# Sliding-window attention into a feed-forward block: one set of eight PSUM banks, score groups of five blocks, and v copies in one piece

## The chip, the core and the metric

The kernel runs on one core of a Trainium2 chip, in one launch. Its time is device microseconds (us). The kernel before was run 11 times: median 265.92 us, from 264.36 to 268.71. The engines are named as the profile names them: PE is TensorE (its matmuls; PEld is its weight loads), DVE is VectorE, ACT is ScalarE, POOL is GpSimd, SP is SyncE.

## What is computed

The reference, cut to what matters (B = 8 batches, H = 8 heads, S = 576 positions, D = 64; 4608 tokens of d_model 512, d_ff 1024):

```
rel = pos[:, None] - pos[None, :]
mask_plain = (rel >= 0) & (rel < 32)                       # heads 0..3
mask_dil = (rel >= 0) & (rel < 128) & (rel % 4 == 0)       # heads 4..7
scores = where(mask, q @ k.T / 8, -1e9)
attn = exp(scores - max);  attn = attn / (sum(attn) + 1e-9)
x = (attn @ v), heads side by side: (4608, 512)
h = (x @ w1) * (x @ w2) @ w3
out = h @ w_out                                            # (4608, 512), f32
```

## The kernel before

**How the work is cut.** Heads 0 to 3 (u=0, plain window) and 4 to 7 (u=1, dilated, rearranged so that its window is plain too) are cut into six blocks of 96 queries, each against 128 keys. Three blocks of four heads are one *step* `b.i` (i = 2u + half), so a batch has four steps and the kernel 32. The feed-forward part takes units of 288 tokens (two per batch, k = 0 to 15), and w3 and w_out are multiplied into one matrix `wf` first, so that a unit needs x@w1, x@w2, their product, and one more matmul.

**The tasks**, with the lines of the profile (line numbers of the kernel before):

- `T`: DVE transposes rows of q, k (and v of batches 0 and 1) into `qt`, `kt`, `vt` (L296, L309).
- `S`: scores on PE into `sp` (L365), 24 matmuls of 32 rows by 96 columns, four at a time in the four row strips of the array. In batches 0 and 1 (`BIASED`) four matmuls first put the mask in as a bias (L348); later batches mask after the exponential.
- `E`: the exponential on ACT, `sp` to `et` (L375). `M`: the mask multiply on DVE (L381), batches 2 to 7.
- `VT`, `VK`: for batches 0 and 1, PE transposes v (L318) and ACT (L329) or DVE (L331) copies it to `vp`, in three pieces per half; `VKE` says which engine. Later batches load v into `vp` by DMA (`LP`, `LD`: L206, L220) and DVE copies the overlap (`HALO`, L227).
- `V`: attention times v on PE, two tasks of 6 matmuls per step (L398). `R`, `N`: reciprocal and normalisation on DVE (L416, L427).
- The result goes to `XT`, transposed: in batches below `TURNED` by PE (`X`, L444) and a copy on ACT (`K`, L451); in the others by a transposing DMA from SP's queue (`XD`, L454).
- `A`, `B`: x@w1 and x@w2 of a unit, 4 matmuls for each of 8 column blocks (L473); `CA` copies A on ACT (L484), `G` multiplies on DVE (L489). `Y`: 8 matmuls per 128 tokens (L500), `CY` copies it on ACT (L511), SP stores it.
- `W3T`, `W3C`, `W3M`, `W3D`: the eight parts of `wf`: transposes (L530), copy on ACT (L537), matmuls (L542), cast on DVE (L552).

**What sets the order.** `Plan.run` is a list planner that runs when the program is built: each task has an engine, a guessed duration, dependencies and a priority (`RANK`, `seq`), and the planner writes the tasks out engine by engine in the order in which its own clock starts them. On the chip every engine then works strictly in that order. Scores of batch b wait for a feed-forward pair that `LEAD` chooses: `pair = int(16 * (b - LEAD) + 4 * i)`.

**PSUM.** It has eight banks. Four are the one tile `sp` for scores, so a step's scores begin only when the exponential before them has read it (`after=[prev["s"]]`). The other four are places `f0` to `f3`, from which the planner gives one to each other PE task (`Plan(places=4)`) until its reader is done.

**Order of loads on POOL's queue:** q, k, v of batch 0; w1, w2; w_out; eight parts of w3; q, k, v of batch 1; then batch 2 and on.

Of the kernel before, what the change touches and what calls it, by code (L numbers as in the profile page):

```python
# [20 lines left out]
D = 64  # L21
# [9 lines left out]
TURNED = 2  # L31
ORDER = (2, 3, 0, 1)
RANK = dict(E=2, VK=1.5, K=1.5, N=0.5, T=3, VT=0.1, S=0.3, V=0.3, X=0.3)
WARM = 16
VKE = (0, 0, 1, 1)
LEAD = 2.25
# [13 lines left out]
class Plan:  # L50
# [5 lines left out]
    def __init__(self, places):  # L56
        self.tasks, self.places, self.now = [], places, None

    def add(self, name, eng, dur, deps, fn, prio, slot=False, lat=150, after=()):
        t = Task(name, eng, dur, deps, fn, prio, slot, lat, after)  # L60
        self.tasks.append(t)
        return t

    def run(self):
# [15 lines left out]
        n, held = len(self.tasks), [None] * self.places  # L80
        now, order, dma = 0.0, [], 0.0

        def freed(t):
            ends = [u.end for u in takers[id(t)]] if t else []
            return None if None in ends else max(ends, default=-200.0) + 100

        while len(order) < n:
            progress = True
            while progress:
                progress = False  # L90
                for e in engines:
                    if free[e] > now:
                        continue
                    at = [freed(t) for t in held]
                    open_ = [(x, i) for i, x in enumerate(at) if x is not None and x <= now]
                    best = None
                    for r, t in waiting[e]:
                        if r > now or (t.slot and not open_):
                            continue
                        if best is None or t.prio < best[1].prio:  # L100
                            best = (r, t)
                    if best is None:
                        continue
                    t = best[1]
                    waiting[e].remove(best)
# [7 lines left out]
                    if t.slot:  # L113
                        t.place = min(open_)[1]
                        held[t.place] = t
# [18 lines left out]
def kernel(  # L134
# [23 lines left out]
    plan = Plan(places=4)  # L158
# [5 lines left out]
    ps_s = ctx.enter_context(tc.tile_pool(name="pss", bufs=1, space=bass.MemoryType.PSUM))  # L164
    ps_f = ctx.enter_context(tc.tile_pool(name="psf", bufs=1, space=bass.MemoryType.PSUM))
# [11 lines left out]
    mask = const.tile([P, 7, QB], BF16, name="mask")  # L177
    vps = [const.tile([P, H, 6, PITCH], BF16, name=f"vp{i}") for i in range(2)]
    bias = const.tile([P, 7, QB], BF16, name="bias")
    ets = [const.tile([P, 4 * VC + 32], BF16, name=f"et{i}") for i in range(4)]  # L180
# [5 lines left out]
    def bank(shape, dtype, name):  # L186
        return ps_f.tile(shape, dtype, tag=f"f{plan.now.place or 0}", name=name)
# [94 lines left out]
    def masks_of_bias():  # L282
        nc.vector.tensor_scalar(
            out=mask, in0=bias, scalar1=0.0, scalar2=None, op0=AL.is_ge
        )
# [27 lines left out]
    def v_back(b, u, half):  # L313
        x = bank([P, 3, 2, P], BF16, "vx")
        for mm in range(3):
            n0 = QB * (3 * half + mm)
            for c in range(2):
                nc.tensor.transpose(  # L318
                    out=x[:, mm, c, :], in_=vts[0][:, u, n0 : n0 + P, c], identity=ident
                )  # L320
        spread[(b, u, half)] = x

    def v_keep(b, u, half, eng):
        dst = vps[b % 2][:, 4 * u : 4 * u + 4, 3 * half : 3 * half + 3, 0:D]
        for mm in range(3):
            o = dst[:, :, mm, :].rearrange("p h (j c) -> p h j c", c=2)
            i = spread[(b, u, half)][:, mm, :, :].rearrange("p c (h j) -> p h j c", h=4)
            if eng == "ACT":
                nc.scalar.copy(out=o, in_=i)  # L329
            else:  # L330
                nc.vector.tensor_copy(out=o, in_=i)  # L331

    class Step:
        def __init__(self, b, u, hf):
            self.b, self.u, self.hf = b, u, hf
            self.et = ets[2 * u + hf]

        def kind(self):
            first = 4 if self.u else self.hf
            return slice(first, first + 3)  # L340

        def scores(self, biased=False):
            b, u, hf = self.b, self.u, self.hf
            qt, kt = qts[b % 2], kts[b % 2]
            self.sp = ps_s.tile([P, 4, 512], F32, tag="s", name="sp")
            if biased:
                for g in range(4):
                    nc.tensor.matmul(  # L348
                        out=self.sp[:, g, 0:VC],
                        lhsT=ident,  # L350
                        rhs=bias[:, self.kind(), :],
# [3 lines left out]
            for mm in range(3):  # L355
                m = 3 * hf + mm
                for c in range(2):
                    for g in range(4):
# [4 lines left out]
                        else:  # L363
                            qq = qt[prt, u, QB * m : QB * m + QB, c]
                        nc.tensor.matmul(  # L365
                            out=self.sp[:, g, QB * mm : QB * mm + QB],
# [3 lines left out]
                            stop=(c == 1 and (mm == 2 or not biased)),  # L370
                        )

        def exps(self):
            ev = self.et[:, 0 : 4 * VC].rearrange("p (g x) -> p g x", g=4)
            nc.scalar.activation(out=ev, in_=self.sp[:, :, 0:VC], func=ACT.Exp, scale=scale)  # L375

        def masks(self):
            ev = self.et[:, 0 : 4 * VC].rearrange("p (g x) -> p g x", g=4)
            mk = mask[:, self.kind(), :].rearrange("p m x -> p (m x)")
            mk = mk.unsqueeze(1).to_broadcast([P, 4, VC])  # L380
            nc.vector.tensor_tensor(out=ev, in0=ev, in1=mk, op=AL.mult)  # L381

        def values(self, pg=None):

            vp = vps[self.b % 2]
            if pg is None:
                o = self.sp[:, :, VC : VC + 3 * (D + 1)].rearrange("p g (m e) -> p g m e", m=3)
                self.o = [o[:, 0:2, :, :], o[:, 2:4, :, :]]
                gs = range(4)
            else:  # L390
                if pg == 0:
                    self.o = [None, None]
                self.o[pg] = bank([P, 2, 3, D + 1], F32, "vo")
                gs = (2 * pg, 2 * pg + 1)
            for g in gs:
                for mm in range(3):
                    c0 = (3 * g + mm) * QB
                    nc.tensor.matmul(  # L398
                        out=self.o[g // 2][:, g % 2, mm, :],
                        lhsT=self.et[:, c0 : c0 + P],  # L400
                        rhs=vp[:, 4 * self.u + g, 3 * self.hf + mm, 0 : D + 1],
# [4 lines left out]
        def recip(self, pg=None):  # L406
            if pg in (None, 0):
                self.rcp = wk_pool.tile([P, 4, 3], F32, tag="rcp", bufs=4, name="rcp")
                self.xo = wk_pool.tile([P, 12 * D], BF16, tag="xo", bufs=4, name="xo")
            if pg is None:  # L410
                o = self.sp[0:QB, :, VC : VC + 3 * (D + 1)].rearrange(
                    "p g (m e) -> p g m e", m=3
                )
                nc.vector.reciprocal(out=self.rcp[0:QB, :, :], in_=o[:, :, :, D])
            else:
                nc.vector.reciprocal(  # L416
                    out=self.rcp[0:QB, 2 * pg : 2 * pg + 2, :], in_=self.o[pg][0:QB, :, :, D]
                )
# [22 lines left out]
        def back(self):  # L441
            self.x = bank([P, 6 * QB], BF16, "x")
# [7 lines left out]
        def keep(self):  # L450
            nc.scalar.copy(out=self.cols(), in_=self.x)  # L451
# [18 lines left out]
    def up(k, f, w_sb, key):  # L470
        ps = bank([P, UNIT], F32, "ab")
        for j, c in enumerate(ORDER):
            nc.tensor.matmul(  # L473
                out=ps,
# [5 lines left out]
        held[(key, k, f)] = ps  # L480

    def copy_a(k, f):
        a_sb = wk_pool.tile([P, UNIT], BF16, tag="asb", bufs=4, name="asb")
# [12 lines left out]
    def down(i):  # L496
        y = bank([P, d_model], F32, "y")
# [29 lines left out]
    def w3_back(ft):  # L527
        x = bank([P, KFF, P], BF16, "x3")
# [10 lines left out]
    def w3_mul(ft):  # L539
        ps = bank([P, d_model], F32, "wf")  # L540
# [256 lines left out]
```

## Time and profile before

The profile is of one execution, which took 264.81 us; its span from first to last instruction is 263.0 us.

| | |
|---|---|
| profiled execution / its span | 264.81 us / 263.0 us |
| median of 11 runs | 265.92 us |
| DMA moved | 32.81 MB, mean 125 GB/s |
| first feed-forward matmul (L473) | at 22.36 us |
| first feed-forward matmul of batch 1 (A2.0) | at 70.24 us |
| last attention matmuls (L398, step 7.3) | at 198.75 us |
| mean granted TensorE clock | 0.994 |

How to read it: the page gives the busy time of each engine, then 40 equal slices of the span with the busy share in tenths, then queues, the chain of work that ended last, and the costliest groups of instructions. A row of a timeline gives start, length, engine, line, operation and tiles, and in brackets the idle time before it and what ended that. Ends of matmuls are modelled and overlap their successors; starts are not, so the pace of PE is read from start to start. The view of waits adds up idle time by the one who ended it. The view of stretches gives busy time by engine in chosen windows, the granted clock and the DMA's share.

### The profile page before, as it was taken

Reading aid. Unit: us, or ns where it says so; the run is one execution under the profiler, and the core shown is the slowest. Engines: PE = TensorE matmul, PEld = TensorE weight load, DVE = VectorE, ACT = ScalarE, POOL = GpSimd, SP = SyncE. Lnnn points to the kernel's source line nnn. Section 1 sums busy time; section 2 is a strip of 40 time slices with the busy share of each in tenths; the row PEclk is TensorE's granted clock in tenths of the full one; section 3 lists DMA queues with packets and bytes.
Section 4 is the critical chain, followed back from the end, with each engine's and each line's share of the span. In section 5 each row is a group of like instructions: output and inputs, shape, how many; then the busy total and the mean of one; then the engine's idle time right before and its main releaser. Section 6 shows DMA issues by size and latency. Waiting matters only on the chain.

```text
span 263.0 us, 6753 instructions
## 1 busy us (share of the span) xinstructions
PE 248.6 (95%) x2706; PEld 168.0 (64%) x2736; DVE 172.5 (66%) x383; ACT 122.2 (46%) x228; POOL 62.6 (24%) x98
## 2 busy tenths in 40 slices
PE   7577999999999999999999999999999999999993
PEld 2355865566667667666667666667676776777661
DVE  4995434899998999989899997455555322233320
ACT  3464454366738354553544545445452342433331
POOL 8621362242635436226313300000000000000000
PEclk9899999999999999999999999999999999999999
DMA  6999999999999969999999944324222111112113
GB/s 97 188 206 207 209 212 211 205 127 167 200 118 165 145 92 210 181 171 181 174 204 123 104 76 65 103 65 65 64 65 62 42 54 67 47 45 72 40 40 120
DMA packets 58030, 32.81 MB, mean 125 GB/s; under 512 B 44688, under 2 KB 47760, under 8 KB 58000
## 3 DMA queue, kind: packets, MB, share of 16 engines
q0 software_dynamic: 37776, 19.40, 58.4%
q1 hardware_dynamic: 20224, 12.98, 23.2%
q8 instruction: 21, 0.34, 0.6%
q14 instruction: 9, 0.07, 0.1%
HBM read 38.80 MB, written 9.44 MB: 183 GB/s over the span
## 4 chain that ended last, share of the span: by engine, by line
PE 80%; DVE 8%; issue 4%; DMA 4%; POOL 1%; ACT 1%; DVEq 0%; POOLq 0%; ACTq 0%
PE ab L473 45%; PE y L500 21%; PE wf L542 5%; PE vo L398 3%; PE sp L365 3%; DMA kn<-in_k_dram 2%; DMA vp<-in_v_dram 2%; DVE xo L427 1%; PE x L530 1%; DVE vt L309 1%; PE sp L348 1%; DVE vt L296 1%; DVE qt L309 1%; DVE gt L489 1%; DVE vp L227 1%
## 5 line engine op out<-in xcount | busy, mean ns | idle before, releaser
L473 PE MATMUL ab<-XT,w_sb 128*128 128x288 bf16 x1024 | 138.0, 286 | 1.3 <-ACT XT L451 0.7
L473 PEld LDWEIGHTS <-w_sb 128*128 128x128 bf16 x1024 | 96.5, 98 | 31.2 <-issue 1.7
L489 DVE TENSOR_TENSOR gt<-ab,asb 128x288 bf16<-128x288 f32 x128 | 57.8, 453 | 58.1 <-PE ab L473 56.2
L484 ACT CAST asb<-ab 128x288 bf16<-128x288 f32 x128 | 51.0, 398 | 50.7 <-PE ab L473 49.7
L500 PE MATMUL y<-wf_sb,gt 128*128 128x512 bf16 x261 | 65.8, 379 | 1.8 <-DVE vp L331 0.5
L511 ACT COPY osb<-y 128x512 f32<-128x512 f32 x36 | 21.1, 585 | 59.3 <-PE y L500 53.9
L500 PEld LDWEIGHTS <-gt 128*128 128x128 bf16 x288 | 27.8, 98 | 28.4 <-DVE vp L331 0.7
L375 ACT ACTIVATE et<-sp 128x1152 bf16<-128x1152 f32 x32 | 36.3, 1134 | 13.7 <-PE sp L365 13.7
L220 POOL DMA_DIRECT2D vp<-in_v_dram x48 | 31.3, 658 | 42.5 <-PE vo L398 17.7
L427 DVE TENSOR_TENSOR xo<-vo,rcp 96x384 bf16<-96x384 f32 x64 | 35.1, 551 | 1.9
L309 DVE STREAM_TRANSPOSE qt<-qn 128x320 uint32<-128x320 uint32 (+1 forms) x32 | 21.5, 680 | 3.2 <-DMA qn<-in_q_dram 2.9
L381 DVE TENSOR_TENSOR et<-et,mask 128x1152 bf16<-128x1152 bf16 x24 | 18.0, 752 | 1.0 <-ACT et L375 0.4
L398 PEld LDWEIGHTS <-et 128*128 128x128 bf16 x384 | 15.9, 99 | 4.4 <-ACT et L375 0.9
L398 PE MATMUL vo<-vp,et 128*128 128x65 bf16 x384 | 17.6, 195 | 0.9 <-ACT et L375 0.8
L416 DVE RECIPROCAL rcp<-vo 96x6 f32<-96x6 f32 x64 | 11.6, 182 | 8.5 <-PE vo L398 8.1
L542 PE MATMUL wf<-wo_sb,w3T 128*128 128x512 bf16 x61 | 14.8, 379 | 0.2
L365 PEld LDWEIGHTS <-kt 32*128 32x128 bf16 x768 | 9.7, 94 | 7.7 <-issue 7.2
L365 PE MATMUL sp<-qt,kt 32*128 32x96 bf16 x768 | 14.3, 204 | 0.1
L537 ACT COPY w3T<-x 128x1024 bf16<-128x1024 bf16 x8 | 8.1, 1012 | 7.7 <-PE x L530 7.6
L309 DVE STREAM_TRANSPOSE kt<-kn 128x320 uint32<-128x320 uint32 (+1 forms) x16 | 10.9, 682 | 0.1
L552 DVE CAST wf_sb<-wf 128x512 bf16<-128x512 f32 x8 | 5.5, 691 | 7.4 <-PE wf L542 7.4
L296 DVE STREAM_TRANSPOSE kt<-kn 128x576 uint32<-128x576 uint32 x8 | 9.9, 1240 | 0.2 <-DMA kn<-in_k_dram 0.2
(46 smaller groups left out, 103.5 us busy)
## 6 DMA issues: line engine op xcount, KB each, us to landing
qn<-in_q_dram POOLq DMA_DIRECT2D x7, 576.0 KB, 9.0
kn<-in_k_dram POOLq DMA_DIRECT2D x7, 576.0 KB, 7.3
w_sb<-in_moe_w_dram POOLq DMA_DIRECT2D x4, 512.0 KB, 12.7
w3n<-in_moe_w_dram POOLq DMA_DIRECT2D x8, 256.0 KB, 14.8
out_dram<-osb SPq DMA_DIRECT2D x8, 256.0 KB, 3.6
out_dram<-osb SPq DMA_DIRECT2D x8, 224.0 KB, 2.4
vp<-in_v_dram POOLq DMA_DIRECT2D x6, 288.0 KB, 11.4
out_dram<-osb SPq DMA_DIRECT2D x8, 192.0 KB, 2.5
```

What stands on the lines that cost most here:

```text
L220: nc.gpsimd.dma_start(out=vp[32 + p0 : 32 + p0 + n, 4:8, m, 0:D], in_=v_rows(b, 4, 4 * t0 + res, [[4 * D, n], [S * D, 4], [1, D]]),)
L309: nc.vector.transpose(out=o, in_=i)
L365: nc.tensor.matmul(out=self.sp[:, g, QB * mm : QB * mm + QB], lhsT=kt[prt, u, QB * m : QB * m + P, c], rhs=qq, start=(c == 0 and not biase ...
L375: nc.scalar.activation(out=ev, in_=self.sp[:, :, 0:VC], func=ACT.Exp, scale=scale)
L398: nc.tensor.matmul(out=self.o[g // 2][:, g % 2, mm, :], lhsT=self.et[:, c0 : c0 + P], rhs=vp[:, 4 * self.u + g, 3 * self.hf + mm, 0 : D + ...
L427: nc.vector.tensor_tensor(out=dst, in0=self.o[pg][0:QB, :, :, 0:D], in1=self.rcp[0:QB, gs, :].unsqueeze(3).to_broadcast([QB, 2, 3, D]), op ...
L473: nc.tensor.matmul(out=ps, lhsT=w_sb[:, c, f * P : (f + 1) * P], rhs=unit_cols(k, c), start=(j == 0), stop=(j == DCH - 1),)
L484: nc.scalar.copy(out=a_sb, in_=held[("a", k, f)])
L489: nc.vector.tensor_tensor(out=gt[:, f, c0 : c0 + UNIT].rearrange("p (r m t) -> p m r t", r=2, m=BLK), in0=held[("b", k, f)].rearrange("p ( ...
L500: nc.tensor.matmul(out=y, lhsT=gt[:, f, c0 : c0 + P], rhs=wf_sb[:, f, :], start=(f == 0), stop=(f == KFF - 1),)
L511: nc.scalar.copy(out=o_sb, in_=held[("y", i)])
L542: nc.tensor.matmul(out=ps, lhsT=w3T[ft][:, g, :], rhs=wo_sb[:, g, :], start=(g == 0), stop=(g == KFF - 1),)
```

## The change

1. PSUM becomes one tile `ps` of eight banks, from which the planner gives one bank to any PE task (`slot=1`) and four, banks 0 to 3 or 4 to 7, to scores (`slot=4`), whichever half is free; while a half is kept for waiting scores no other task gets banks of it. The rule that scores wait for the exponential before them is gone.
2. `Step` is split: a `Group` makes scores, exponential and masks. In batches 0 and 1 a group is three blocks as before. From batch 2 a group is five blocks, running on across steps and batches (72 blocks: 14 groups of five and one of two). The mask multiply of a group is two tasks, one for each pair of heads, and a `V` task waits for its own pair's mask alone. A step whose blocks lie in two groups waits for both.
3. `v_keep` copies a half in one instruction. Of the copies of batches 0 and 1 only `VK1.0.1` is on DVE (before: four of eight halves).
4. `TURNED` is 1: the results of batch 1 go through the transposing DMA. Of the `K` copies of batch 0, two (`K0.2`, `K0.3`) go to DVE.
5. The masks are made by five POOL instructions that stand on POOL's queue after q and k of batch 2 and ahead of its v, not by one DVE instruction at the start.
6. Two of the eight parts of w3 are loaded after q, k, v of batch 1. `RANK`, `LEAD`, the number of warming matmuls (16 to 18) and of `asb` buffers (4 to 6) change.

```diff
-TURNED = 2
+TURNED = 1
-RANK = dict(E=2, VK=1.5, K=1.5, N=0.5, T=3, VT=0.1, S=0.3, V=0.3, X=0.3)
-WARM = 16
-VKE = (0, 0, 1, 1)
-LEAD = 2.25
+RANK = dict(E=1, VK=1, K=0.4, N=1.5, T=3, VT=0.4, S=0.4, V=0.4, X=0.1)
+WARM = 18
+W3_FIRST = 6
+ON_DVE = ("K0.2", "K0.3", "VK1.0.1")
+GRP = 5
+LEAD = 1.7
...
+        def place(t):
+            nonlocal kept
+            ok = [x is not None and x <= now for x in map(freed, held)]
+            if t.slot == 4:
+                halves = [h for h in (0, 4) if all(ok[h : h + 4])]
+                if halves:
+                    return halves[0]
+                if kept is None:
+                    kept = max((0, 4), key=lambda h: sum(ok[h : h + 4]))
+                return kept if all(ok[kept : kept + 4]) else None
+            at = [i for i in range(8) if ok[i] and (kept is None or i // 4 != kept // 4)]
+            if not at:
+                return None
+            used = [4 - sum(ok[h : h + 4]) for h in (0, 4)]
+            return max(at, key=lambda i: (used[i // 4], -freed(held[i])))
...
-    plan = Plan(places=4)
+    plan = Plan()
-    ps_s = ctx.enter_context(tc.tile_pool(name="pss", bufs=1, space=bass.MemoryType.PSUM))
-    ps_f = ctx.enter_context(tc.tile_pool(name="psf", bufs=1, space=bass.MemoryType.PSUM))
+    ps_pool = ctx.enter_context(tc.tile_pool(name="ps", bufs=1, space=bass.MemoryType.PSUM))
+    ps = ps_pool.tile([P, 8, 512], F32, name="ps")
...
-    mask = const.tile([P, 7, QB], BF16, name="mask")
+    mask = const.tile([P, 16, QB], BF16, name="mask")
-    ets = [const.tile([P, 4 * VC + 32], BF16, name=f"et{i}") for i in range(4)]
+    ets = [const.tile([P, 4 * GRP * QB + 32], BF16, name=f"et{i}") for i in range(4)]
...
     def masks_of_bias():
-        nc.vector.tensor_scalar(
-            out=mask, in0=bias, scalar1=0.0, scalar2=None, op0=AL.is_ge
-        )
+        for at, first, n in ((0, 0, 4), (4, 1, 2), (6, 4, 3), (9, 4, 3), (12, 0, 4)):
+            nc.gpsimd.tensor_scalar(
+                out=mask[:, at : at + n, :],
+                in0=bias[:, first : first + n, :],
+                scalar1=0.0,
+                scalar2=None,
+                op0=AL.is_ge,
+            )
...
     def v_keep(b, u, half, eng):
-        for mm in range(3):
-            o = dst[:, :, mm, :].rearrange("p h (j c) -> p h j c", c=2)
-            i = spread[(b, u, half)][:, mm, :, :].rearrange("p c (h j) -> p h j c", h=4)
+        o = dst.rearrange("p h m (j c) -> p m h j c", c=2)
+        i = spread[(b, u, half)].rearrange("p m c (h j) -> p m h j c", h=4)
...
+    class Group:
+        def __init__(self, i, blocks):
+            self.blocks, self.n, self.et = blocks, len(blocks), ets[i % len(ets)]
+        def scores(self, biased=False):
+            self.sp = ps[:, plan.now.place : plan.now.place + 4, :]
...
+        def exps(self):
+            x = self.n * QB
+            ev = self.et[:, 0 : 4 * x].rearrange("p (g x) -> p g x", g=4)
+            nc.scalar.activation(out=ev, in_=self.sp[:, :, 0:x], func=ACT.Exp, scale=scale)
+        def masks(self, half):
+            x = self.n * QB
+            ev = self.et[:, 2 * half * x : 2 * (half + 1) * x].rearrange("p (g x) -> p g x", g=2)
...
-        a_sb = wk_pool.tile([P, UNIT], BF16, tag="asb", bufs=4, name="asb")
+        a_sb = wk_pool.tile([P, UNIT], BF16, tag="asb", bufs=6, name="asb")
...
-    mk = add("masks", "DVE", 700, [blk], masks_of_bias, 40, lat=80)
+    mk = add("masks", "DMA", (2500, 0), [blk], masks_of_bias, 26.5, lat=-1800)
...
+    loads_w3(range(W3_FIRST))
+    for nm in ("qn", "kn", "vn"):
+        loads_rows(nm, 1)
+    loads_w3(range(W3_FIRST, KFF))
...
+            todo += every
+            while len(todo) >= GRP or (todo and b == B - 1):
+                group(todo[:GRP], False)
+                todo = todo[GRP:]
```

The order that comes out, as the built program has it. PE, start: `S0.0 S0.1 VT VT S0.2 S0.3 V0.0 V0.1 VT VT X0.0 V0.2 X0.1 V0.3 X0.2 A0.0 B0.0 X0.3 A0.1 ...`. PE, from unit 1 to unit 2: `... W3M4 W3M5 B1.5 A1.6 S1.0 S1.1 S1.2 S1.3 VT VT VT VT W3T6 V1.1 V1.0 V1.2 W3T7 W3M6 V1.3 W3M7 B1.6 A1.7 B1.7 Y0 Y1 A2.0 ...` (before: `... W3M7 S1.0 A1.5 Y0 VT VT S1.1 VT VT V1.0 Y1 V1.1 S1.2 X1.0 B1.5 A1.6 X1.1 S1.3 V1.2 B1.6 A1.7 B1.7 V1.3 S2.0 X1.2 Y2 X1.3 S2.1 A2.0 ...`). DVE, start: all transposes of batch 0, then `R`/`N` of steps 0.0 to 0.2 and the first half of 0.3, `K0.2`, `R0.3.1 N0.3.1 G K0.3`. ACT: `E0.0 E0.1 VK VK E0.2 E0.3 VK K0.0 VK K0.1 CA ...`, and for batch 1 `E1.0 E1.1 E1.2 E1.3 VK VK W3C6 VK W3C7`. SP: `XD1.1 XD1.0 XD1.2 XD1.3`, then stores.

## The prediction

> **What bounds the kernel now.** I read the page first, for the engine that is full:
>
> ```profile
> span 263.0 us, 6753 instructions
> PE 248.6 (95%) x2706; PEld 168.0 (64%) x2736; DVE 172.5 (66%) x383; ACT 122.2 (46%) x228; POOL 62.6 (24%) x98
> PE   7577999999999999999999999999999999999993
> DVE  4995434899998999989899997455555322233320
> ```
>
> PE is below 9 tenths only in the first 4 slices (26 us) and the last. There DVE shows 9: two places with different limits. DVE is full again from slice 9 to 23, though PE stays at 9. The stretches say how full PE is:
>
> ```profile
> 6.00:12.00 6.00, 2.77 (x44) 1.97 (x43) 5.43 (x9) 2.15 (x5) 4.52 (x7) 0.90 1.02 178
> 12.00:18.00 6.00, 4.79 (x104) 3.39 (x102) 5.48 (x14) 3.64 (x6) 1.61 (x3) 0.81 1.21 202
> 53.00:70.24 17.24, 16.59 (x302) 11.45 (x302) 16.63 (x37) 11.46 (x21) 8.48 (x12) 1.00 1.21 166
> 70.24:150.00 79.76, 78.39 (x1002) 53.62 (x1007) 73.67 (x161) 40.96 (x74) 32.15 (x45) 1.00 1.35 158
> ```
>
> Columns are PE, PEld, DVE, ACT, POOL busy, clock, DMA share, GB/s. From 70 to 150 us PE is busy 98% and DVE 92%. Ends of matmuls are modelled, so I take PE's pace from starts in a timeline:
>
> ```profile
> 106.70 0.44 PE L365 MATMUL sp<-qt,kt 32*128 32x96 bf16 x24
> 107.08 2.13 PE L473 MATMUL ab<-XT,w_sb 128*128 128x288 bf16 x16
> 109.14 0.45 PE L365 MATMUL sp<-qt,kt 32*128 32x96 bf16 x24
> 109.52 0.54 PE L398 MATMUL vo<-vp,et 128*128 128x65 bf16 x12
> ```
>
> Sixteen feed-forward matmuls take 16 x 0.122 = 1.95 us (starts 0.122 apart inside every run of them). From 107.08 that ends at 109.03, but the scores begin at 109.14: **0.10 us is lost on entering scores**. Inside scores starts come 0.0105 apart on the mean, 23 x 0.0105 = 0.24, yet the next kind starts 0.38 after the first score: **0.12 are lost on leaving**. Both recur at nearly every group of scores with no wait beside it. By the same reading of starts, over all PE, 17 of the 263 us are not matmul pace: about 10.5 before the first feed-forward matmul at 22.36, 6.5 after. Of the 6.5, some 2.9 are true waits after 70 us, the rest mostly these entries and exits.
>
> So the time is PE's work, plus a start of 22.36 us that DVE sets, plus 4 us of end (last copy and store, unchanged). An edit counts if it takes work from PE, shortens the start, or makes or ends a wait on PE.
>
> **The change, part by part.**
>
> *Groups of five.* Before, 24 unbiased groups cost 0.38 + 0.10 = 0.48 each: 11.5 us. A group of five has 40 matmuls: 0.48 + 16 x 0.0105 = 0.65; 14 of them and one of 16 matmuls (0.39) make 9.5. **-2.0 us**, all on PE. Lower bound 0 (if the loss came from something that grows with the matmuls), upper 2.2. The biased groups keep their switches.
>
> *Batch 1 through the transposing DMA.* Four `X` of 6 transposes go from PE:
>
> ```profile
> 63.62 0.42 PE L444 MATMUL x<-ident,xo 96*128 96x96 bf16 x6
> 63.88 0.66 PE L348 MATMUL sp<-bias,ident 128*128 128x288 bf16 x4
> ```
>
> 0.26 from start to start, 4 x 0.26: **-1.0 us**. Four `K` of 0.64 leave ACT, which was 46% busy. What comes instead is below.
>
> *The start.* `A0.0` begins when the `XT` of steps 0.0 to 0.2 are there. The transposes are held by the landings (q 5.47, k 7.07, v 9.1, then 10.5, 11.9, about 13.4), and that doesn't change; the mask instruction taken off DVE (0.55) filled a landing gap. After: the k transposes end at 13.34 as before; `S0.2` and `S0.3` (0.96 each from start to start with bias) need no exponential before them and run to 15.3; `V0.0` stands behind them, so the first reciprocal comes at about 15.7, when all transposes are done (13.4 + 1.3 = 14.7). Before it came at 13.63, but then v transposes (1.40) and six v copies (2.07) stood between the pairs. Now pairs of `R` and `N` follow each other every 0.70: six to 19.9, `X0.2` on PE to 20.3, one more pair on DVE to 20.6, `K0.2` 0.45 to 0.75 (576 elements; rows 512 in 0.69 and 288 in 0.45), `A0.0` at 21.3 against 22.36: **-1.0**. Bounds: -1.6, if PE's clock stays whole, to +0.6, if a v copy on ACT is late.
>
> That clock: granted 0.90 and 0.81 in the first two stretches above, that is half rate from 10.8 to 14.2. By the Trainium skill (TensorE: Matmul & The Clock Gate, part 1) the gate closes after an idle window of about 3.4 us. Here it closed though PE paused only from 6.2 to 8.55 and worked again, so the row decides, and I count half rate again for parts of the start. By the rule the gate would stay open and the start be some 0.5 us shorter.
>
> *v copies in one piece.* Before, three pieces took 1.76/2 = 0.88 on ACT and 1.04 on DVE per half. A line through ACT's copies (288 elements 0.398, 1024 in 1.012: 0.16 + 0.00083 each) gives 0.80 for 768. At most 0.1 each, on engines beside PE: **0**, except in the passage below.
>
> *Masks on POOL.* DVE loses 0.55. POOL's nearest rows, affine selects of 48 and 96 columns at 0.225 and 0.278, give 1.1 ns a column: 5 instructions, 1536 columns, 1.1 (fixed part alone) to 2.6 us. I take 2.6. They delay v of batch 2, whose loads were issued from 37.4 to 56.6 and are first read at 68.9 with no DMA wait named: **0**, until the delay passes about 5 us. By the Trainium skill (SBUF, "Who interferes with whom") a GpSimd instruction that reads SBUF and a DVE one with two SBUF inputs shut each other out; that speaks against the move, but these fall near 40 us, where DVE gates and casts from PSUM, one SBUF input at most. No row here shows such a blocking.
>
> *Mask multiplies.* 752 ns for 1152 columns; half a group is 960, about 650. 29 or 30 of them make 19.0 us against 18.0. DVE is +1.0 here and -3.5 in v copies and the mask: **0**.
>
> *The passage from unit 1 to unit 2.* Here waits are added. After, PE comes to `S1.0` at 21.3 + 0.3 + 12.2 (100 matmuls) + 15.0 (six `W3T` of 0.45, six `W3M` of 1.73, 16 of 0.122) = 48.8. The transposes of batch 1 are ready: its rows stand two loads of 256 KB further ahead, 2.5 us at 208 GB/s. Up to `A2.0` PE has 4 x 0.96, 24 x 0.056, 2 x 0.45, 2 x 1.73, 48 x 0.03, 12 x 0.122, 2 x 1.73 = 15.9 us. But scores stand together, so ACT has four exponentials (1.13 each) in a row, to 54.5, and then three v copies (0.85) and two `W3C` (1.01), to 59.2; `W3M7` waits for the last, so `A2.0` is reached at 66.0: 1.3 us of waits. And `A2.0` needs `XD1.2`. On DVE, 7 `R`, 6 `N` and a cast stand between 56.0 and the end of `N1.2.1`: 61.2. SP issues transposes 1.2 us each, so `XD1.2` starts at 61.7. How long it takes:
>
> ```profile
> DMA to landing us min/median/max: 2.3/4.2/9.8
> ```
>
> The low values come where little is loaded; between 100 and 150 us it was 5.9 to 9.8, at 72 to 84, beside v of batch 3 as here, 2.3 to 6.0. I take 5.3: `A2.0` at 67.0. Behind it on PE stand all of unit 2, `S2.0` and `Y2`, and nothing else can be taken; on SP three stores stand behind the transposes, for which nobody waits. Before, it stood at 70.24, but by then `Y2` (1.73) and two groups of scores (0.96) were done as well: comparable 67.55. So 0.55 of the 2.0 won by `X` and the start remains: **+1.5**, from 0 to +5.5.
>
> *Other waits, LEAD, eight banks, six `asb` buffers.* 2.9 us of waits after 70 us; I leave them: **0**, from -2 (DVE lighter, scores don't wait for an exponential) to +6 (below).
>
> Sum: -2.0 - 1.0 - 1.0 + 1.5 = **-2.5 us**. Against the profiled execution (264.81) that is 262.3. It lies 1.1 below the median of 265.92, so the forecast for a median is **263.4**, -0.9%. A measurement of this kernel can tell about 0.5% (1.3 us) from no change: below 264.6 is faster, above 267.2 slower.
>
> **Rivals.**
>
> 1. *The transposes of batch 1 land late.* For: POOL's loads of v of batch 3 start when `V1.3` is done, just when these go out. Against: 4.6 was the median at 72 to 84. With the 7.3 of the busy stretch, PE waits 2.0 more at `A2.0`: 265.4, no change. 15%.
> 2. *The loss at scores isn't a loss per group.* Then the 2.0 stay away: 265.4. Against: 0.10 and 0.12 recur beside different neighbours. 10%.
> 3. *The long exponential starves the feed-forward matmuls* (slower). By the same line a five-block exponential is 0.16 + 1920 x 0.00083 = 1.78 us against 1.13. `CA` (0.40) stands behind it on ACT, and with four banks PE has 4 x 0.49 = 1.96 us of `A` and `B` before it needs the bank that `CA` frees. Before: 1.13 + 0.40 + 0.1 = 1.63, covered. After: 2.28, 0.35 too late, 0.8 where the bank is one that `G` frees. At 0.35 for 15 groups 5.3 us: 268.7. It decides from 0.17 us per group. Against: `Y` (1.73) stands among these matmuls in many places, and of eight banks some of the other half are free once `V` is done. 12%.
> 4. *More waits go.* If half of the 2.9 goes and `XD1.2` lands after 4.2: 260.9. 13%.
>
> Forecast 50%. Faster: nearly all of the forecast's 50, rival 4, a little of 1 and 2: 0.62. Same: 0.24. Slower: rival 3 and the end of rival 1: 0.14. The range runs from 260.6 to 267.4: it takes in rivals 1, 2 and 4 and leaves out rival 3 and a transposing DMA at its worst.
>
> **What would show it.** PE starts around scores: 40 matmuls in 0.55 and 0.10 ahead of them; 15 unbiased groups. `A0.0` near 21.3, after `K0.2`. `A2.0` near 67, its wait named by the `XT` transpose; if by 69 or later, rival 1. Waits on PE after 70 us near 3 us; if 8, with ACT's exponential ahead of `CA`, rival 3. POOL's five mask instructions under 3 us. I am wrong if the last score groups come so late that units near the end wait for `XT`, or if eight banks in one tile make waits that the bank order doesn't ask for.

## The result, and the profile after

| | before | after |
|---|---|---|
| median (lowest to highest) | 265.57 us, 48 runs (264.26 to 275.78) | 267.27 us, 13 runs (265.94 to 268.18) |
| profiled execution / its span | 264.81 / 263.0 us | 267.86 / 265.7 us |
| A0.0 / A2.0 on TensorE | 22.36 / 70.24 us | 21.11 / 70.80 us |
| mean granted TensorE clock | 0.994 | 0.985 |

The ratio of after to before is **1.0069, 95% interval 1.0045 to 1.0093**: a loss of 0.7%, small, but clear of no change. Forecast was a gain, 263.4. The page of after, the rows that answer to those shown of before, and the clock:

```profile
span 265.7 us, 6709 instructions
PE 247.5 (93%) x2684; PEld 168.2 (63%) x2714; DVE 169.0 (64%) x383; ACT 119.2 (45%) x208; POOL 66.7 (25%) x103
PE   8678999998399999999999999999999999999993
PEclk9999999999779999999999999999999999999999
```

TensorE is busy 1.1 us less, and its start is fuller (8, 6, 7, 8 against 7, 5, 7, 7). But the eleventh slice, from 66.4 to 73.1 us, now shows 3, and the clock shows 7 in it and in the next. Before, the clock was whole there:

```profile
PEclk9899999999999999999999999999999999999999
```

The view of waits of TensorE, the largest (us in all, times, longest); the next one is 1.5, in the start:

```profile
PE ps L492 <- DMA XT<-xo: 5.1, 1, 5.1
```

One wait of 5.1 us, of the first unit of batch 1 (L492 is the feed-forward line) for a transposing DMA. The stretches, columns as in the prediction:

```profile
53.00:70.00 17.00, 12.46 (x130) 7.96 (x131) 11.10 (x26) 6.65 (x10) 8.19 (x12) 1.00 1.27 137
66.60:70.00 3.40, 0.00 (x0) 0.00 (x0) 0.00 (x0) 0.00 (x0) 0.58 (x1) 1.00 1.60 155
70.00:76.80 6.80, 5.78 (x58) 3.45 (x60) 2.86 (x5) 2.57 (x3) 1.39 (x2) 0.50 1.49 165
```

From 66.6 to 70.0 no engine shows any work but one instruction of POOL, and for the next 6.8 us the clock is granted at half. The timeline around it says what waits and what went out at the same time:

```profile
57.34 0.72 POOL L219 DMA_DIRECT2D qn<-in_q_dram  x1 [0.18 <-DVE rcp L432]
57.58 9.47 SPq L473 DMA_TRANSPOSE XT<-xo  x4
58.06 0.73 POOL L219 DMA_DIRECT2D kn<-in_k_dram  x1
58.77 1.21 POOL L227 DMA_DIRECT2D vp<-in_v_dram  x1
...
62.12 3.62 PE L519 MATMUL ps<-wf_sb,gt 128*128 128x512 bf16 x15
...
70.80 1.62 PE L492 MATMUL ps<-XT,w_sb 128*128 128x288 bf16 x6 [5.07 <-DMA XT<-xo]
```

The four transposes of batch 1 stand on SP's queue from 57.58. POOL begins to issue q, k and v of batch 3 within the same microsecond and a half. After its last `Y` TensorE has nothing that it may take until the transposes land.

### The profile page after: what moved, and what is told of

Its sections match the earlier page's. It is cut to its first block, busy times and chain, and to the rows that moved or that the text cites. A ratio compares the mean times of both kernels' runs of the same rounds, so it can differ in the third digit from the quotient of the medians.

```text
span 265.7 us, 6709 instructions
## 1 busy us (share of the span) xinstructions
PE 247.5 (93%) x2684; PEld 168.2 (63%) x2714; DVE 169.0 (64%) x383; ACT 119.2 (45%) x208; POOL 66.7 (25%) x103
## 4 chain that ended last, share of the span: by engine, by line
PE 82%; DMA 9%; DVE 4%; issue 1%; POOL 1%; ACT 1%; POOLq 0%; DVEq 0%; ACTq 0%
PE ps L492 48%; PE ps L519 22%; PE ps L561 4%; PE ps L420 4%; DMA XT<-xo 4%; PE ps L387 3%; DMA vp<-in_v_dram 3%; DMA qn<-in_q_dram 2%; DVE xo L443 2%; PE ps L549 1%; DVE qt L336 1%; DVE kt L336 1%; DVE wf_sb L571 0%; ACT et L398 0%; DVE rcp L432 0%
## 5 line engine op out<-in xcount | busy, mean ns | idle before, releaser
L492 PE MATMUL ps<-XT,w_sb 128*128 128x288 bf16 x1024 | 138.5, 288 | 6.0 <-DMA XT<-xo 5.1
L492 PEld LDWEIGHTS <-w_sb 128*128 128x128 bf16 x1024 | 98.1, 98 | 36.9 <-DMA XT<-xo 5.6
L508 DVE TENSOR_TENSOR gt<-ps,asb 128x288 bf16<-128x288 f32 x128 | 58.0, 455 | 67.1 <-PE ps L492 65.6
L503 ACT CAST asb<-ps 128x288 bf16<-128x288 f32 x128 | 50.7, 398 | 70.4 <-PE ps L492 65.2
L519 PE MATMUL ps<-wf_sb,gt 128*128 128x512 bf16 x261 | 65.7, 381 | 1.5 <-issue 0.2
L530 ACT COPY osb<-ps 128x512 f32<-128x512 f32 x36 | 21.1, 585 | 54.8 <-PE ps L519 51.3
L398 ACT ACTIVATE et<-ps 128x1920 bf16<-128x1920 f32 (+2 forms) x23 | 34.2, 1505 | 8.9 <-PE ps L387 8.3
L443 DVE TENSOR_TENSOR xo<-ps,rcp 96x384 bf16<-96x384 f32 x64 | 34.0, 543 | 0.9
L406 DVE TENSOR_TENSOR et<-et,mask 128x960 bf16<-128x960 bf16 (+1 forms) x30 | 17.8, 627 | 2.4 <-ACT et L398 2.4
L420 PE MATMUL ps<-vp,et 128*128 128x65 bf16 x384 | 16.7, 193 | 1.0 <-ACT vp L355 0.7
L561 PE MATMUL ps<-wo_sb,w3T 128*128 128x512 bf16 x61 | 14.6, 379 | 0.2
L387 PEld LDWEIGHTS <-kt 32*128 32x128 bf16 x768 | 9.5, 94 | 7.2 <-issue 4.9
L387 PE MATMUL ps<-qt,kt 32*128 32x96 bf16 x768 | 12.9, 205 | 1.0 <-DVE kt L336 1.0
```

Of the source, the lines that this page charges most:

```text
L387: nc.tensor.matmul(out=self.sp[:, g, QB * i : QB * i + QB], lhsT=kt[prt, u, QB * m : QB * m + P, c], rhs=qq, start=(c == 0 and not biased) ...
L398: nc.scalar.activation(out=ev, in_=self.sp[:, :, 0:x], func=ACT.Exp, scale=scale)
L420: nc.tensor.matmul(out=self.o[pg][:, g % 2, mm, :], lhsT=grp.et[:, c0 : c0 + P], rhs=vps[self.b % 2][:, 4 * self.u + g, 3 * self.hf + mm, ...
L443: nc.vector.tensor_tensor(out=dst, in0=self.o[pg][0:QB, :, :, 0:D], in1=self.rcp[0:QB, gs, :].unsqueeze(3).to_broadcast([QB, 2, 3, D]), op ...
L492: nc.tensor.matmul(out=o, lhsT=w_sb[:, c, f * P : (f + 1) * P], rhs=unit_cols(k, c), start=(j == 0), stop=(j == DCH - 1),)
L503: nc.scalar.copy(out=a_sb, in_=held[("a", k, f)])
```

## The experiments

**Theory L (landing):** the loss is this wait and the half clock behind it, both made by `TURNED = 1`; the rest of the change is a gain. **Rival:** the loss lies in the eight banks, the long exponentials or the planner's new order.

### The second turn back on TensorE

```diff
-TURNED = 1
+TURNED = 2
```

> The changed kernel with TURNED back at 2: the results of batch 1 are turned by PE again, all else stays and the planner orders it anew. Theory L (the whole loss is the landing of batch 1's transposing DMAs, 9.3 to 10.2 us each, which leaves PE idle 5.1 us ahead of A2.0, and the half clock from 70.0 to 76.8 us that follows that idle time and costs some 3 us): both are gone, PE gets 1.0 us of transposes more, so 267.3 - 5.1 - 3.0 + 1.0 = about 260, granted clock 0.99. Rival W (the time is held by DVE and by the long exponentials; the idle time at A2.0 only shows where it gathers): the waits come back elsewhere after 70 us, 265 to 267.

Measured: 260.46 us (260.05 to 261.16), ratio to before **0.9816 [0.9774, 0.9857]**. Its largest waits of TensorE:

```profile
PE ps L580 <- DVE warm L583: 1.2, 1, 1.2
PE ps L492 <- DVE rcp L432: 0.8, 1, 0.8
```

All are in the start; from 60 us on the view names no wait of TensorE at all. One line of the change turned a gain of 1.8% into a loss of 0.7%.

### The same line alone, in the kernel before

```diff
-TURNED = 2
+TURNED = 1
```

> The kernel before with TURNED = 1 alone: batch 1 through the transposing DMA in the old order, all else as before; the planner orders it anew. Theory L (the DMA for batch 1 is what costs, wherever the rest stands): PE saves 1.0 us of transposes, but waits at A2.0, so 266 to 271 against 264.9. Rival (the cost comes only with the new order, in which v of batch 3 and q, k go out at that moment): 264, 1.0 us less.

Measured: 272.57 us, ratio 1.0265 [1.0215, 1.0315], +7.0 us; in after the line costs 267.27 - 260.46 = 6.8. Its wait and its clock row:

```profile
PE ab L473 <- DMA XT<-xo: 5.0, 1, 5.0
...
PEclk9979999999869999999999999999999999999999
```

Its four transposes land after 6.0 to 9.2 us. So the loss needs neither the eight banks nor the groups of five: it comes with the line into a kernel without them.

### The idle stretch filled, the wait left as it is

22 unused matmuls, whose product nobody reads, between the last `Y` and `A2.0`:

```diff
+    def fill():
+        o = bank(512)
+        for i in range(22):
+            nc.tensor.matmul(out=o, lhsT=warm[:, 0:P], rhs=warm, start=True, stop=True)
...
+        if i == 1:
+            add("FILL", "PE", 1, [y], fill, -1000, slot=1)
```

> The changed kernel with 22 matmuls on the warming tile, whose result nobody reads (22 x 0.216 = 4.75 us), put on PE between Y1 and A2.0, where it idles 5.1 us; every order is otherwise the same. Theory L: A2.0 starts when it did (70.5 to 71.2) since the landing hasn't changed, but the clock stays full, so about 3 us less: 264.3, clock 0.99. Rival W: the half clock costs nothing because PE isn't what holds the time there: 267 as before.

Measured: 264.67 us (10 runs), ratio 0.9999 [0.9971, 1.0026]. The stretch after the wait, columns as before:

```profile
70.00:76.80 6.80, 6.69 (x128) 4.55 (x127) 4.96 (x9) 4.48 (x6) 2.10 (x3) 1.00 1.37 158
```

`A2.0` starts at 70.12, 0.7 us sooner, but the clock is whole and 128 matmuls start in the 6.8 us instead of 58. **The half clock costs about 267.27 - 264.67 = 2.6 us**, half the length of the wait of 5.1, on top of it. The profiled executions agree: after is 0.7 us behind this one at `A2.0` and 3.5 at the end of the span (265.7 against 262.2), so 2.8 us are lost behind the wait. The ratios, each to the runs of before beside it, give 0.7% or 1.9 us.

### q and k of batch 3 loaded later

The two loads are moved behind the v pieces of their batch on POOL's queue:

```diff
+    late = [t for t in order if t.name in ("Lqn3", "Lkn3")]
+    order = [t for t in order if t not in late]
+    at = [t.name for t in order].index("LD3.5") + 1
+    order[at:at] = late
```

> The changed kernel with one thing moved: on POOL's queue the loads of q and k of batch 3 stand behind the loads of v of batch 3, not ahead of them; the order on every other engine is the same. Theory L with its cause (packets of 256 bytes of the transposes take turns with packets of 2304 bytes of q and k, some 200 ns each): the transposes of batch 1 land in 3 to 6 us, A2.0 starts by 67.5. Rival D (the transposes are slow by themselves or behind each other, or any loads slow them as much): they still take 9 to 10 us and A2.0 starts at 70 to 71. The total is left open, since q and k of batch 3 come later here and may make another wait.

The transposes of batch 1 from issue to landing, first in after, then here:

```profile
DMA to landing us min/median/max: 9.3/9.6/10.2
```

```profile
DMA to landing us min/median/max: 4.7/5.1/6.6
```

`A2.0` starts at 67.13, after 0.45 us of waiting, and the clock stays whole there. The time is 264.22 (one run). So q and k beside the transposes are what makes them late. The trace's packet records say how: the transposes move in packets of 256 bytes, 31 ns each. In after, from 62 to 66 us, 77 to 93 of them per us get through beside 74 to 79 packets of q and k, 2304 bytes and 191 ns each; from 67 to 71 us, beside 413 to 424 of v's packets of 128 bytes (31 ns), it is 393 to 407 per us. The counts of the two queues are alike in both stretches: there **it is packet against packet, whatever their size**. Here, with only small packets beside them, it is 130 to 650 per us, and the counts aren't alike (131 beside 954 in one of these microseconds), so one for one is a reading of those two stretches alone. What the run didn't settle: the full gain of `e1` doesn't come, since k and q of batch 3 now arrive late. DVE waits for q, the `G` behind it (L508) is late, and TensorE waits for that:

```profile
75.92 0.73 DVE L336 STREAM_TRANSPOSE qt<-qn 128x320 uint32<-128x320 uint32 x1 [3.40 <-DMA qn<-in_q_dram]
...
76.99 1.26 PE L492 MATMUL ps<-XT,w_sb 128*128 128x288 bf16 x9 [2.86 <-DVE gt L508]
```

### The planner told how late the transposes land

```diff
-                x = add("XD" + n, "SP", 100, ns, st.back_dma, 0, lat=3700)
+                x = add("XD" + n, "SP", 100, ns, st.back_dma, 0, lat=9500 if bb == 1 else 3700)
```

> The changed kernel with one number changed: the planner is told 9500 ns, not 3700, for the landing of batch 1's transposes. It then puts Y2, S2.0, Y3 and S2.1 ahead of A2.0 (1.73 + 0.65 + 1.73 + 0.65 = 4.8 us of work into the 5.1 us of idle time). Theory L: the transposes still land in 9 to 10 us, PE waits under 1 us at A2.0, the clock stays full, 267.3 - 4.5 - 3.0 = about 260. Rival W: 264 to 267.

Measured: 268.21 us, ratio 1.0104 [1.0058, 1.0151]: a miss by 8 us, no better than after. The planner did fill the gap, with `Y` and scores of batch 2. The timeline around 74 us says what came instead:

```profile
74.06 0.58 ACT L530 COPY osb<-ps 128x512 f32<-128x512 f32 x1 [3.35 <-DMA out_dram<-osb]
74.54 1.78 ACT L398 ACTIVATE et<-ps 128x1920 bf16<-128x1920 f32 x1
...
74.70 0.65 PE L492 MATMUL ps<-XT,w_sb 128*128 128x288 bf16 x4 [2.05 <-ACT osb L530]
```

A copy of `Y` on ACT waits 3.35 us for an output buffer: there are three, and the store that empties one stands on SP's queue behind the transposes (the first is issued at 66.9 us, and they take up to 7.6 us to land). The exponential behind the copy waits too, and so does TensorE, first for the copy's bank (2.05 us), then for the exponential; its clock halves again, from 76.8 to 80.2. **Theory S:** the order is good, and the stores are what is short.

### The same with a fourth output buffer

```diff
-    w3_pool = ctx.enter_context(tc.tile_pool(name="w3", bufs=8))
+    w3_pool = ctx.enter_context(tc.tile_pool(name="w3", bufs=7))
...
-        o_sb = wk_pool.tile([P, d_model], F32, tag="osb", bufs=3, name="osb")
+        o_sb = wk_pool.tile([P, d_model], F32, tag="osb", bufs=4, name="osb")
...
-                 after=[stores[-3] if len(stores) > 2 else None])
+                 after=[stores[-4] if len(stores) > 3 else None])
```

> e4 (planner told 9500 ns, 268.2 us) with one more buffer for the stores: osb 4 instead of 3, paid for by w3 7 instead of 8; the order on PE and ACT around A2.0 is the same as in e4. Theory S (in e4 the copy of Y3 on ACT waited 3.4 us for a store that stood on SP's queue behind the transposes of batch 1, with the exponential of S2.1 behind it on ACT, so that A2.1 waited for a bank): that wait goes, and the half clock from 76.8 to 80.2 us with it, 262 to 264. If e4 was slow for another reason, 267 to 268.

Measured: ratio 0.9889 [0.9826, 0.9952], median 262.86, as theory S has it. The profiled execution is the slowest of the four (266.78 us, the others 261.87 to 263.54). It has two long waits between 104 and 110 us (1.1 and 3.1 us) and a halved clock behind them, so it is read from 60 to 100 us alone: there TensorE waits for no copy of `Y`, and the clock is whole. With the wait planned for and a fourth buffer the transposing DMA is affordable. Its median is 2.4 us above that of four groups of transposes on TensorE, but the intervals (0.9826 to 0.9952 and 0.9774 to 0.9857) overlap, so that it is worse isn't established.

### Groups of three instead of five

In the kernel with the second turn on TensorE:

```diff
-GRP = 5
+GRP = 3
```

> The changed kernel with TURNED = 2 (the kernel of e1, 260.5 us) and groups of three blocks instead of five, so 24 unbiased score groups and not 15. Prediction's term (0.10 us on entering and 0.12 on leaving scores, per group): 9 groups x 0.22 = 2.0 us more, 262.5. Rival 2 (the loss grows with the matmuls, not with the groups): 260.5. Rival 3 (long exponentials starve the feed-forward matmuls, so short ones help): below 260.

Measured: 263.71 us, ratio 0.9949 [0.9922, 0.9977], +3.2 us. The switches that I counted explain 2.0. Its waits from 60 to 230 us hold 1.8 us for exponentials (L492 1.4, L387 0.4), which groups of five don't have.

### The old LEAD

In the same kernel:

```diff
-LEAD = 1.7
+LEAD = 2.25
```

> The kernel of e1 with LEAD back at 2.25, so that scores are released as early as in the kernel before. The waits on PE after 70 us (2.9 us in the kernel before) are nearly gone in e1. If the later release took them away, they are back: 262 to 263.5. If it was the one set of banks and the lighter DVE, no change: 260.5.

Measured: 262.04 us (261.27 to 265.25), ratio 0.989 [0.9847, 0.9934]. Inconclusive: the interval overlaps that of the second turn's kernel (0.9774 to 0.9857) by 0.001, both profiled spans are 259.2 (with a mean clock of 1.0 here and of 0.993 there, so the equal spans hide some of a difference), and 1.8 us of waits of TensorE for exponentials come back, the longest 1.3.

### The old split of the banks

In the kernel with the second turn on TensorE, the planner gives scores banks 4 to 7 alone, and everything else banks 0 to 3:

```diff
-                halves = [h for h in (0, 4) if all(ok[h : h + 4])]
-                if halves:
-                    return halves[0]
-                if kept is None:
-                    kept = max((0, 4), key=lambda h: sum(ok[h : h + 4]))
-                return kept if all(ok[kept : kept + 4]) else None
-            at = [i for i in range(8) if ok[i] and (kept is None or i // 4 != kept // 4)]
+                return 4 if all(ok[4:8]) else None
+            at = [i for i in range(4) if ok[i]]
```

> The kernel with the second turn on TensorE, its planner held to the split of before: scores in banks 4 to 7 alone, everything else in banks 0 to 3; the order of the work follows from that. Theory (the one set of eight banks is worth something by itself, in the start and where the work passes from one batch to the next, since the first scores take their bank at once): +1 to +2.5 us, 261.5 to 263 us. Rival (the split cost nothing, the gain of the rest of the change came from elsewhere): 260.5 us, no change that can be told.

Measured: 269.73 us, ratio 1.017 [1.0118, 1.0221]: +9.3 us, nearly four times the most that the theory had. The start is part of it (`A0.0` at 22.82 instead of 20.75), but more is in the long middle: at the 257th of the 1024 matmuls of `A` and `B` this kernel is 3.7 us behind the one with one set (98.7 against 95.0 us), at the 769th 8.3 (210.4 against 202.1). The stretch from 100 to 220 us, first in the kernel with one set, then with the split:

```profile
100.00:220.00 120.00, 120.00 (x1349) 83.23 (x1346) 85.84 (x198) 56.15 (x103) 21.73 (x31) 1.00 0.77 110
```

```profile
100.00:220.00 120.00, 117.24 (x1298) 79.81 (x1295) 82.44 (x190) 53.55 (x98) 20.00 (x30) 1.00 0.70 105
```

51 matmuls fewer in 120 us. The waits of TensorE there, from 100 to 205 us, name the normalisation (L438) and A's copy:

```profile
PE ps L487 <- DVE xo L438: 1.4, 4, 0.3
PE ps L415 <- ACT asb L498: 0.7, 2, 0.4
```

The view counts from modelled ends. From start to start, as in the prediction, delays of over 0.15 us between 70 and 205 us add up to 6.2 us here and to none in the kernel with one set. The largest stand where `A` follows value tasks (L415), for instance:

```profile
146.16 0.71 PE L415 MATMUL ps<-vp,et 128*128 128x65 bf16 x18
147.17 0.34 PE L415 MATMUL ps<-vp,et 128*128 128x65 bf16 x6 [0.30 <-DVE gt L503]
147.85 1.19 PE L487 MATMUL ps<-XT,w_sb 128*128 128x288 bf16 x8 [0.34 <-DVE xo L438]
```

L487 is `A` and `B`, whose operands don't come from the normalisation of that moment, so I take it to wait for a bank. At 146.16 us three value tasks (18 matmuls) come one behind the other and a fourth soon after, as a group of five allows, and each holds one of four banks until DVE has normalised it, while `A` and `B` need the same four. From this I formed the theory that **groups of five and the one set need each other**.

### The old split and groups of three

```diff
-GRP = 5
+GRP = 3
```

on top of the split.

> The kernel with the second turn on TensorE, with both the split of the banks and groups of three blocks, as before; what is left of the change is the rest of it (the start, the order, masks on GpSimd, six buffers for A). It closes the square of the two: one set and groups of five 260.5, one set and groups of three 263.7, split and groups of five 269.7. Theory (the two need each other: under the split a score group of five delivers two or three value steps at once to four shared banks, and each then waits 0.3 to 0.5 us for a bank; groups of three ask for fewer at a time): 264 to 267 us, about the time of before. Rival (the two add up): 269.7 + 3.2 = 273 us.

Measured: 265.86 us, ratio **0.9999 [0.9971, 1.0028]**: the time of before. The same stretch:

```profile
100.00:220.00 120.00, 119.94 (x1358) 81.88 (x1357) 88.98 (x209) 58.42 (x109) 20.08 (x30) 1.00 0.75 107
```

The view of waits names none in it. The square (medians in us; second turn on TensorE in all):

| | groups of three | groups of five |
|---|---|---|
| split of four and four | 265.86 | 269.73 |
| one set of eight | 263.71 | 260.46 |

Under the split, groups of five lose 3.9; in one set they win 3.2 (by the ratios to before 1.7% and 1.3%). That the two need each other is shown; that banks held by value tasks are the way is read from the rows above. And what the change holds besides these two and `TURNED` is, under the split and with groups of three, together worth nothing that can be told: with both undone it stands at before.

### The v copies in three pieces again

In the kernel with the second turn on TensorE:

```diff
-        o = dst.rearrange("p h m (j c) -> p m h j c", c=2)
-        i = spread[(b, u, half)].rearrange("p m c (h j) -> p m h j c", h=4)
-        if eng == "ACT":
-            nc.scalar.copy(out=o, in_=i)
-        else:
-            nc.vector.tensor_copy(out=o, in_=i)
+        for mm in range(3):
+            o = dst[:, :, mm, :].rearrange("p h (j c) -> p h j c", c=2)
+            i = spread[(b, u, half)][:, mm, :, :].rearrange("p c (h j) -> p h j c", h=4)
+            if eng == "ACT":
+                nc.scalar.copy(out=o, in_=i)
+            else:
+                nc.vector.tensor_copy(out=o, in_=i)
```

> The kernel with the second turn on TensorE, the copies of v and k in three pieces again as before, the orders otherwise the same. A copy in one piece took 0.80 us on ScalarE, three pieces of before took 0.88 in sum. Theory (the copies stand beside other work): +0.0 to +0.3 us, 260.5 to 260.8 us, not to be told from no change. Rival (a copy in one piece lets the bank go later, or sooner, than the work behind it needs): more than 0.7 us either way.

Measured: 260.92 us, ratio 0.9838 [0.9779, 0.9897], not to be told from 0.9816.

### The gaps of the start filled

The kernel with the second turn on TensorE, with 11 unused matmuls in gaps of the start:

```diff
+    def fill(n):
+        o = bank(512)
+        for i in range(n):
+            nc.tensor.matmul(out=o, lhsT=warm[:, 0:P], rhs=warm, start=True, stop=True)
+    FILL = {"VT0.0.1": 4, "X0.0": 2, "X0.1": 2, "X0.2": 3}
```

> The kernel with the second turn on TensorE, and 11 unused matmuls put into TensorE's idle gaps of the start (4 behind the transposes of v, 2 behind each of the first two X turns, 3 behind the third). In that kernel's profile the clock was granted at half from 20.6 to 24.0 us, after a stretch of 3.41 us in which TensorE was busy for 0.36 of the time, and this cost about 1.6 us. Theory (the clock gate closes after 3.41 us in which TensorE was busy below about 0.43, not only after an idle stretch): with the filling every such stretch is above that, the clock is whole throughout, A of batch 0 still begins at about 20.8, and the time is 259 to 260.5 us. Rival (the filling stands in the way of the first real matmuls, or the gate closes all the same): 260.5 us or more.

Measured: **259.79 us (259.58 to 259.98), ratio 0.9784 [0.9747, 0.982]**, the fastest of all. First the clock row of the kernel without the filling, then with it:

```profile
PEclk9997999999999999999999999999999999999999
```

```profile
PEclk9999999999999999999999999999999999999998
```

The intervals with and without the filling overlap, so the 0.7 us between the medians is not established by them. The spread is narrower: without it four runs had clocks of 0.993 (261.16, 260.74) and 1.0 (260.19, 260.05); with it all six are 0.997 or more and lie within 0.4 us. That fits the theory, by which the filling takes away the executions in which the clock halves in the start, but two of four against none of six doesn't establish it.

## Why the prediction was wrong

**The step that failed is the landing of batch 1's transposes:** "How long it takes [...] I take 5.3: `A2.0` at 67.0." The four took 9.3 to 10.2, `XD1.2` 9.4, and `A2.0` started at 70.80. TensorE was done with what stands ahead at 65.6 (forecast 66.0), and `XD1.2` was issued at 61.38 (forecast 61.7), so the times around the step were right. The range that I quoted (2.3 to 9.8) all but held the answer; I picked the row by the wrong likeness, "beside v of batch 3 as here". What stood beside it was q and k of batch 3 as well, with packets nine times as large as the transposes'. The packet records of before could have told me: while its three transposes of that row (72 to 84 us) were under way, no packet of q or k was; in after 227 to 512 were during each. I had the rival (number 1) with 15%, and priced it with 7.3 of landing, 2.0 us; its end was 5.1.

**The step that was missing is the clock.** I reckoned with half rate in the start and nowhere else. A wait of 5.1 us, with a whole window of 3.4 us without matmuls in it, brought 6.8 us at half rate: about 2.6 us, which no term of the sum held. I took a wait as if it cost its own length.

These two alone would have made 263.4 + 3.8 (`A2.0` at 70.80, not 67.0) + 2.6 = 269.8. That it was 267.27 goes with gains that I had too small: waits that went and groups of five, below.

The other steps:

| step | forecast | measured |
|---|---|---|
| `A0.0` | 21.3, -1.0 | 21.11, but with the clock whole, for which I had -1.6: in part luck; 22.7 and 22.8 with the split, whose profiled clock halved ahead of it, so how much comes from the one set isn't shown |
| groups of five | -2.0, at best -2.2 | -3.2 in one set, +3.9 under the split |
| `X` off TensorE | -1.0 | not measured alone; the whole line costs +6.8 |
| waits after 70 us | 2.9, unchanged | gone in the kernel with the second turn: this half of rival 4 came |
| exponential of 1920 columns | 1.78 us | 1.77; rival 3 didn't come |
| mask multiply of 960 | 0.65 | 0.646 |
| v copy in one piece | 0.80 on ACT, 0 in the sum | 0.82; 0.5 between the medians, not resolved |
| LEAD | 0 | -1.6, not resolved |

Scores do cost what I read from starts, for instance in after (the next kind starts at 101.90, 0.55 after the first of 40; 12 of L492 ahead of them take 12 x 0.122 = 1.46 of 1.56, so 0.10 on entering):

```profile
99.79 1.63 PE L492 MATMUL ps<-XT,w_sb 128*128 128x288 bf16 x12
101.35 0.62 PE L387 MATMUL ps<-qt,kt 32*128 32x96 bf16 x40
```

One term was set at nothing without a reason: the eight banks. They are worth -2.2 with groups of three and -9.3 with groups of five; the square shows that neither they nor the groups of five are a term of their own.

Some small readings of the prediction are off, without weight in the sum: 0.16 + 1920 x 0.00083 is 1.75, not 1.78, and 2.28 - 1.96 is 0.32, not 0.35; what is lost on leaving scores is 0.13, not 0.12; five fixed parts of a mask instruction are 0.9, not 1.1; and in the first four slices DVE shows 4, 9, 9, 5, so it is full in two of them.

The ledger in medians: 267.27, less 2.6 for the clock (between medians), less about 5.1 for the wait (the profile's row), plus about 1.0 for the `X` that go back (worked out, not measured) makes 260.6; 260.46 was measured. That it closes so well is in part luck, since the clock's term may be anything from 1.9 to 2.8. Two things stay open: why the total with q and k late is 264.2 and not lower is read from one profile only, and `LEAD` isn't settled.

## What to carry to other kernels

Before work is moved to a DMA, look up which transfers will stand beside it and compare packet sizes, not bytes: here a transfer of small packets got no more packets through than the large ones beside it. Price a long wait of TensorE with the half clock that follows (here waits of 3.1 and 5.1 us brought it, as did waits of 2.0 and 1.0 us close together; one of 2.9 us did not), and look whether anything is left that may be run in it. Buffers and the size of the work that they carry are one choice: try each pair of them, since here either half of a good pair alone was worth less, and one of them was a loss.

## What the runs showed of the hardware

**The clock.** By the Trainium skill (TensorE: Matmul & The Clock Gate, part 1) the gate closes after an idle window of about 3.4 us. The stretch in after agrees (0.00 busy from 66.6 to 70.0). But less than idleness is enough. I laid windows of 3.41 us, in step with the changes of the granted clock, over all traces but that of the fourth buffer, from where the clock is on record (4 to 7 us) to 245 us. TensorE's busy share is reckoned from starts: each matmul counts from its start for its pace (0.216 us for 512 columns, 0.122 for 288, in proportion for fewer, twice that at half rate), and overlaps count once. The clock halved after windows of 0.00, 0.19, 0.26, 0.31, 0.31, 0.32, 0.33, 0.36, 0.42 and 0.43, and stayed whole after every window of 0.44 and more. In the trace left out it halved after 0.18 and stayed whole after 0.43. So the bound lies at about 0.43 of a window; this is a reading of these traces, and the filled start is the one experiment that was built on it. At half rate it mostly came back after one window (TensorE busy 0.78 to 1.00 of it). In after it took two, though TensorE was busy 0.76 of the first; whether that is the bound for coming back, these runs don't tell.

It also goes with the spread from run to run. Before was run beside the other kernels in four sets: the runs with a mean clock of 1.0 have medians of 264.4 to 264.6 us by set, those with 0.993 or 0.994 265.4 to 265.6, those with 0.987 266.9 to 267.3.

**GpSimd's mask instructions** took 704 ns for 192 columns, about 935 for 288 and 1165 to 1200 for 384: 2.4 ns a column and 0.24 us. All five took 4.8 us, where I had at most 2.6 from affine selects, and "under 3 us" as a sign. They moved the loads behind them, and nothing waited for it. The two casts of DVE that ran beside them took 0.69 us, as before; no DVE instruction with two inputs from SBUF ran at that time, so the blocking that I weighed wasn't put to the test.
